# Splitting the expert weights once, and giving each weight slot its own run of tiles

## The chip, the cores and the metric

The kernel runs on one core of a Trainium2 chip. The core has a matrix engine (PE; its weight loads are listed as PEld), a vector engine (DVE), an activation engine (ACT), GpSimd (POOL) and a sync engine (SP) that mostly issues transfers. Each engine works through its own queue in order, and waits on semaphores where another engine or a transfer has to be done first. The metric is the device time of one execution in microseconds (us).

## The reference, cut to what matters

```python
# convolution along the sequence, by FFT of double length: x (8, 5696, 128), h (5696, 128)
y = irfft(rfft(x, 2*S, axis=1) * rfft(h, 2*S, axis=0)[None])[:, :S]
x = y.reshape(45568, 128)
# one expert of eight per token
logits = x @ w_gate + modality_bias[modality_id]
e_idx = argmax(logits, axis=1)
gate_w = softmax(logits)[range(N), e_idx]
for e in range(8):                      # w1[e]: 128 x 1024, w2[e]: 1024 x 128
    mask = e_idx == e
    out[mask] = gate_w[mask, None] * (maximum(x[mask] @ w1[e], 0) @ w2[e])
```

All arrays are float32. The kernel gets float32 accuracy from products in a shortened float32 format (float32r) by splitting an operand into a high part (a cast) and a low part (the rest), and adding three products: high by high, high by low, low by high. For the expert weights this split is what the change is about.

## The kernel before, in words

The convolution is a transform in four stages, over two groups of four batches. Stage 1 (`stage1`) transforms over 64 points and writes to a scratch in memory. Stages 2 and 3 (`stage23`, one step per k of 64) transform over the residues, multiply by the filter's transform and go back, into the scratches ua and ub. Stage 4 (`stage4`) goes back over k, three pairs of residues at a time; it makes the logits, picks the expert, ranks the tokens within their expert, and hands each of twelve columns of 128 tokens to `dispatch`, an indirect transfer from POOL (L297) that scatters the rows into `rows`, a scratch with a region for each expert.

The experts (`class Moe`) then work on tiles: 512 consecutive rows of one expert, or 256 in the last level. There are four levels, of 18, 18, 45 and 23 tiles: those that are full for sure after 27 pairs of residues of the first group, after the whole first group, after all, and then the short rest. For each level `table` works out on one partition, with small DVE operations, the first row and the expert of every tile and a flag that says whether the expert differs from that of the tile NSLOT places before. `load` brings a tile's rows (mrt, five buffers), and waits on SP for the scatters of the tile whose buffer it takes. `load_weights` reads the expert and the flag into registers of SP and loads 1 MiB of raw weights (w1 and w2 of the expert side by side) into one of two buffers raw, only if the flag is set. `split` makes the high part (ACT, L520) and the low part (DVE, L522; in the last level half of them on POOL) of a quarter of the weights, into one of three buffers slot; four such steps lie beside each tile's products, for the tile after it, whether raw was loaded anew or not. `prep` transposes the rows and splits them. `gemm1` makes the hidden rows (PE L546 to L548, ACT hh L551, DVE hl L552), `gemm2` the output (PE L568 to L570) two steps later, `finish` transposes back, multiplies by the gate (DVE L584) and scatters to out from POOL (L587).

A tile has eight steps (four if short), written out in `Moe.run`. `run_all` interleaves generators step by step: stages 2 and 3 of the first group with stage 1 of the second; stages 2 and 3 of the second group with stage 4 of the first 27 pairs; then the rest of stage 4 with the tiles. The framework's scheduler orders each engine's queue from this by priority and a simulated timeline, ahead of the run; only SP keeps the written order during the experts.

Of the kernel before, what the change touches and what calls it, by code (L numbers as in the profile page):

```python
# [10 lines left out]
F32 = mybir.dt.float32  # L11
F32R = mybir.dt.float32r
BF16 = mybir.dt.bfloat16
I32 = mybir.dt.int32
# [7 lines left out]
E, FF = 8, 1024  # L22
# [12 lines left out]
QA = 27     # pairs of residues of the first group that are dispatched before the experts start  # L35
HP = 1000   # how far the routing moves up in the scheduler's order
PACE = 2    # dispatches queued behind each product's last sum
S4R = 5     # steps of stage 4 per three of stages 2 and 3
RATE = 1.05  # steps of stage 4 per step of the experts
WH = 2      # every WH-th product goes back through whole float32 matmuls, the others through split ones  # L40
W0 = 52     # ... in the first group from this one on
LG = 3      # every LG-th set of logits goes through split operands
AHEAD = 6   # steps of stage 4 before the first fence


def full(q):
    """Tiles of TS rows that the tokens of the first q pairs of residues, over the groups' batches, fill for sure."""
    return (GB * (128 * q - 64) - E * (TS - 1)) // TS


# Tiles by level: full ones after a part of the first group, after the first group, after all, then short ones.
# [9 lines left out]
NSLOT = 2  # L61
# [3 lines left out]
def run_all(*gens):  # L65
    """Emit generators side by side; each is (generator, steps it takes per round)."""
    live = [[g, float(r), 0.0] for g, r in gens]
    while live:
        for it in list(live):
            it[2] += it[1]  # L70
            while it[2] >= 1.0:
                it[2] -= 1.0
                try:
                    next(it[0])
                except StopIteration:
                    live.remove(it)
                    break
# [3 lines left out]
def conv_moe(  # L81
# [3 lines left out]
    zd, hd, ua, ub, rows_d, out,  # L85
# [349 lines left out]
    def table(tp, lv, before):  # L435
# [17 lines left out]
        # Row of tile t of expert e: cur[e] + ts * (t - cum[e]), as a sum of steps at the experts' first tiles.  # L453
# [4 lines left out]
        it_i = t_(nt, "it_i", I32)  # L458
        nc.gpsimd.iota(it_i, pattern=[[1, nt]], base=0, channel_multiplier=0)
        it = t_(nt, "it")  # L460
        nc.vector.tensor_copy(it, it_i)
# [21 lines left out]
        if not last:  # L483
            # Rows of each expert in the first nt tiles.
            nc.vector.tensor_scalar(cum, cum, float(nt), None, op0=ALU.min)
            nc.vector.tensor_tensor(cnt, cum[:, 1:], cum[:, :E], op=ALU.subtract)
            nc.vector.scalar_tensor_tensor(cur, cnt, float(ts), cur, op0=ALU.mult, op1=ALU.add)
# [4 lines left out]
    class Moe:  # L492
        def __init__(self, wp, sp, pst, psh, pso):
            self.sp, self.pst, self.psh, self.pso = sp, pst, psh, pso
            self.raw = [wp.tile([128, 2, FF], F32, name=f"raw{i}") for i in range(NSLOT)]
            self.slots = [wp.tile([128, 2, 2, FF], F32R, name=f"slot{i}") for i in range(3)]
            self.st = {}
            self.tabs = {}
# [11 lines left out]
        def load_weights(self, t):  # L510
# [4 lines left out]
            nc.sync.dma_start(self.raw[t % NSLOT], w12_d[bass.ds(ex, 1)].rearrange("o p a f -> (o p) a f"), cond=ch > 0)  # L515

        def split(self, t, k):
            raw, w = self.raw[t % NSLOT], self.slots[t % 3]
            i, fs = k // 2, slice(k % 2 * (FF // 2), (k % 2 + 1) * (FF // 2))
            nc.scalar.copy(w[:, i, 0, fs], raw[:, i, fs])  # L520
            eng = nc.gpsimd if JOBS[t][0] == len(LEVELS) - 1 and k % 2 else nc.vector
            eng.tensor_tensor(w[:, i, 1, fs], raw[:, i, fs], w[:, i, 0, fs].bitcast(F32), op=ALU.subtract)  # L522
# [14 lines left out]
        def gemm1(self, t, f):  # L537
            w = self.slots[t % 3]
# [16 lines left out]
        def gemm2(self, t, f):  # L555
            w = self.slots[t % 3]
# [34 lines left out]
        def run(self):  # L591
# [11 lines left out]
            for k in range(4):  # L603
                self.split(0, k)
            self.prep(0)
            for g in range(len(steps) + LAG):
# [5 lines left out]
                if f == 0 and t + 2 < total:  # L612
                    self.load_weights(t + 2)
                if t < total:
                    self.gemm1(t, f)
                if g >= LAG:
                    self.gemm2(*steps[g - LAG][:2])
                if t + 1 < total:
                    if n == 4 or f % 2 == 1:
                        with tc.issue_after(self.st[t]["act"].ins):  # L620
                            self.split(t + 1, f * 4 // n)
# [12 lines left out]
    with tc.tile_pool(name="p4", bufs=2, space=PSUM) as ps4, \  # L634
            tc.tile_pool(name="p4l", bufs=1, space=PSUM) as ps4l:
        with tc.tile_pool(name="s2", bufs=2) as sp2, tc.tile_pool(name="p2x", bufs=3, space=PSUM) as psx, \
# [6 lines left out]
            run_all((stage23(1, sp2, psx, psu), 3), (stage4(0, sp4, ps4, ps4l, 0, QA, True), S4R))  # L643
            dispatch(len(queue))

        def fence():
            """Orders the loads of a level behind the dispatch before it."""
# [113 lines left out]
```

## Time and profile before

| | us |
|---|---|
| median of three timed runs | 2400.83 (2379.54 to 2401.71) |
| span of the profiled execution, first to last instruction | 2272.4 |
| own time of the profiled execution | the page gives only its span |
| mean granted clock of PE | 0.955 |
| busy: PE, DVE, ACT, POOL | 2068.7, 1751.5, 1394.7, 1242.3 |

On the trace's own clock stage 1 of the first group runs until about 236 us, stages 2 and 3 of the first group with stage 1 of the second until about 560, stages 2 and 3 of the second group with the first part of stage 4 until about 890, tiles beside the rest of stage 4 until about 1420, full tiles alone until about 2070 to 2095, and the 23 short tiles to the end.

How to read the lines that follow. The table of windows has a row for each stretch: its ends and length, then busy time and count of instructions for each engine, the granted clock (1.00 is full), the busy share of the transfer engines and their rate in GB/s. A group of instructions has the line, the engine, the operation, the tiles out<-in with their shapes and the count; then busy time, mean ns of one, idle time of the engine ahead of them and what ended it. A tile's row has the shortest, median and longest duration in ns, and the first and last start. A wait has who waited, for whom, the sum in us, how many times and the longest. A row of the timeline or of the chain has its start, its length in us and what ran; SPq is SP's queue.

### The profile page before, as it was taken

How to read it: one execution, taken by the hardware profiler on the slowest of the kernel's cores; microseconds unless marked ns; L12 is line 12 of the kernel's file. 1: busy time of each engine (PE TensorE's matmuls, PEld its weight loads, DVE VectorE, ACT ScalarE, POOL GpSimd, SP SyncE). 2: the span in 40 equal slices, each digit the busy share in tenths (PEclk: the TensorE clock that was granted, in tenths of full speed). 3: DMA queues.
4: the chain of work that ended last, by engine and by line, in shares of the span. 5: the costliest groups of instructions: out<-in, count | busy, mean ns of one | idle time of the engine just before them, and what ended most of it. 6: DMA issues, size and time to landing. Idle time of an engine off the chain costs nothing. (4 is left out here: it accounts for less than half of the span.)

```text
span 2272.4 us, 33999 instructions
## 1 busy us (share of the span) xinstructions
PE 2068.7 (91%) x9752; PEld 1537.7 (68%) x9752; DVE 1751.5 (77%) x2907; ACT 1394.7 (61%) x2496; POOL 1242.3 (55%) x1102
## 2 busy tenths in 40 slices
PE   6779899899888988989888998999999999999896
PEld 5655555445554545877766776888888888888886
DVE  6559999899889896778566777877777777777675
ACT  6547776546444545766666664666666666666674
POOL 2126665664787887754777777333333333334675
PEclk9999999899979996999999999999999999999998
DMA  9989989778767766443445423232112211112321
GB/s 325 332 294 314 325 287 297 209 243 273 219 190 212 219 196 205 142 135 100 139 123 160 147 83 103 81 100 64 47 60 63 65 62 44 46 43 90 127 81 46
DMA packets 195436, 357.48 MB, mean 157 GB/s; under 512 B 32438, under 2 KB 63514, under 8 KB 191409
## 3 DMA queue, kind: packets, MB, share of 16 engines
q1 hardware_dynamic: 150560, 270.52, 37.3%
q0 software_dynamic: 23520, 47.61, 6.3%
q10 hardware_dynamic: 21168, 37.17, 5.4%
q8 instruction: 78, 1.28, 0.2%
q14 instruction: 110, 0.89, 0.1%
HBM read 276.51 MB, written 157.43 MB: 191 GB/s over the span
## 5 line engine op out<-in xcount | busy, mean ns | idle before, releaser
L552 DVE SCALAR_TENSOR_TENSOR hl<-ph,hh 128x512 fp32r<-128x512 f32 x740 | 508.2, 689 | 257.6 <-ACT hh L551 248.9
L587 POOL DMA_INDIRECT out<-of,mrt x370 | 390.2, 1055 | 535.8 <-DVE of L584 427.2
L551 ACT ACTIVATE hh<-ph 128x512 fp32r<-128x512 f32 x740 | 443.1, 600 | 362.7 <-PE ph L548 354.8
L297 POOL DMA_INDIRECT rows<-rt,idx x360 | 401.7, 1116 | 121.6 <-issue 85.8
L270 POOL TENSOR_TENSOR t<-t,t 96x512 f32<-96x512 f32 x218 | 335.5, 1560 | 182.5 <-DVE t L263 163.4
L263 DVE TENSOR_TENSOR t<-px,hs 96x512 f32<-96x512 f32 x512 | 320.2, 675 | 26.0 <-ACT hs L223 10.5
L546 PE MATMUL ph<-mxh,slot 128*128 128x512 f32 (+1 forms) x832 | 322.1, 387 | 16.8 <-DVE hl L552 13.1
L568 PE MATMUL po<-hh,slot 128*128 128x512 f32 (+1 forms) x832 | 326.6, 393 | 9.5 <-ACT hh L551 9.3
L548 PE MATMUL ph<-mxh,slot 128*128 128x512 f32 (+1 forms) x832 | 312.4, 376 | 0.6 <-POOL slot L522 0.4
L569 PE MATMUL po<-hl,slot 128*128 128x512 f32 (+1 forms) x832 | 311.0, 374 | 0.0
L547 PE MATMUL ph<-mxl,slot 128*128 128x512 f32 (+1 forms) x832 | 310.8, 374 | 0.0
L570 PE MATMUL po<-hh,slot 128*128 128x512 f32 (+1 forms) x832 | 310.5, 373 | 0.0
L260 PE MATMUL px<-z,m 96*96 96x512 f32 x512 | 269.9, 625 | 21.6 <-issue 6.6
L522 DVE TENSOR_TENSOR slot<-raw,slot 128x512 fp32r<-128x512 f32 x370 | 265.3, 719 | 22.6 <-ACT slot L520 22.4
L520 ACT CAST slot<-raw 128x512 fp32r<-128x512 f32 x416 | 251.8, 614 | 23.8 <-DMA raw<-in_w 23.8
L546 PEld LDWEIGHTS ph<-mxh,slot 128*128 128x128 f32 x832 | 159.5, 192 | 43.3 <-DVE hl L552 18.3
L243 ACT COPY ut<-pu 90x512 f32<-90x512 f32 x256 | 144.5, 583 | 70.0 <-PE pu L238 25.8
L568 PEld LDWEIGHTS po<-hh,slot 128*128 128x128 f32 x832 | 159.1, 191 | 33.2 <-ACT hh L551 10.8
L548 PEld LDWEIGHTS ph<-mxh,slot 128*128 128x128 f32 x832 | 158.7, 191 | 31.6 <-POOL slot L522 0.8
L569 PEld LDWEIGHTS po<-hl,slot 128*128 128x128 f32 x832 | 158.7, 191 | 30.0 <-DVE hl L552 0.2
L570 PEld LDWEIGHTS po<-hh,slot 128*128 128x128 f32 x832 | 158.8, 191 | 29.6
L547 PEld LDWEIGHTS ph<-mxl,slot 128*128 128x128 f32 x832 | 159.1, 191 | 26.7
(153 smaller groups left out, 3477.8 us busy)
## 6 DMA issues: line engine op xcount, KB each, us to landing
raw<-in_w SPq DMA_DIRECT2D x104, 1024.0 KB
z<-z SPq DMA_DIRECT2D x256, 180.0 KB
z<-z SPq DMA_DIRECT2D x90, 320.0 KB
z<-z SPq DMA_DIRECT2D x90, 256.0 KB
ua<-ut SPq DMA_DIRECT2D x128, 180.0 KB
ub<-ut SPq DMA_DIRECT2D x128, 180.0 KB
mrt<-rows SPq DMA_DIRECT2D x81, 260.0 KB
u<-ua ACTq DMA_DIRECT2D x63, 256.0 KB
```

The source lines that it names most:

```text
L263: nc.vector.tensor_tensor(prod[i, j].rearrange("p (b d) -> p b d", d=D), px[:KP].rearrange("p (b d) -> p b d", d=D), hs[:, j, k % KH].unsq ...
L270: add = eng.tensor_tensor(y[:, i], y[:, i], prod[1, 1 - i], op=ALU.add if i else ALU.subtract)
L297: nc.gpsimd.indirect_dma_start(views[count[0] % NVIEW], bass.IndirectOffsetOnAxis(ap=idx[:, t:t + 1], axis=0), rt[:, t, :], None, bounds_c ...
L546: nc.tensor.matmul(po, w[:, 0, 0, fs], st["xh"], start=True, stop=False)
L547: nc.tensor.matmul(po, w[:, 0, 0, fs], st["xl"], start=False, stop=False)
L548: nc.tensor.matmul(po, w[:, 0, 1, fs], st["xh"], start=False, stop=True)
L551: st["act"] = nc.scalar.activation(hh, ph, AF.Relu)
L552: nc.vector.scalar_tensor_tensor(hl, ph, 0.0, hh.bitcast(F32), op0=ALU.max, op1=ALU.subtract)
L568: nc.tensor.matmul(po, w[:, 1, 0, fs], hh[:, cs], start=k == 0, stop=False)
L569: nc.tensor.matmul(po, w[:, 1, 0, fs], hl[:, cs], start=False, stop=False)
L570: nc.tensor.matmul(po, w[:, 1, 1, fs], hh[:, cs], start=False, stop=k == 7)
L587: nc.gpsimd.indirect_dma_start(oviews[(t * NSUB + c) % NVIEW], bass.IndirectOffsetOnAxis(ap=ri[:, c, D + 1:D + 2], axis=0), of[:, c, :], N ...
```

## The change

Between stages 2 and 3 of the second group and stage 4, a third generator, `presplit`, is interleaved, one step per round: in 16 steps (eight experts, w1 and w2) it loads 512 KiB of raw weights, casts the high part on ACT, subtracts on DVE and stores both parts, 1 MiB, to a new scratch w12s; its tile has one buffer, and ACT issues both transfers. `load_weights` now loads 2 MiB of ready parts from w12s straight into the slot, if the expert of the slot changes; raw and `split` are gone. NSLOT, the distance of the flag's comparison, goes from 2 to 3, so a slot keeps its weights from one of its tiles to the next. `table` numbers the tiles of a level in another order: tile j of the level is number (j % 3) * run + j // 3, with run the third part of the level's tiles rounded up, so each slot walks through a contiguous run of the experts. The call of `load_weights(t + 2)` moves from ahead of `gemm1` at step 0 of tile t to behind `gemm2` at step 1, where `gemm2` has just read the slot for the last time for tile t - 1.

```diff
-NSLOT = 2
+NSLOT = 3
...
-    zd, hd, ua, ub, rows_d, out,
+    zd, hd, ua, ub, rows_d, w12s, out,
...
+    def presplit(sp):
+        for e in range(E):
+            for a in range(2):
+                s = sp.tile([128, 2, FF], F32R, name="ws")
+                v = s.bitcast(F32)
+                nc.scalar.dma_start(v[:, 1], w12_d[e, :, a])
+                nc.scalar.copy(s[:, 0], v[:, 1])
+                nc.vector.tensor_tensor(s[:, 1], v[:, 1], v[:, 0], op=ALU.subtract)
+                nc.scalar.dma_start(w12s[e, :, a], v)
+                yield
...
-        it_i = t_(nt, "it_i", I32)
-        nc.gpsimd.iota(it_i, pattern=[[1, nt]], base=0, channel_multiplier=0)
+        it_i = t_(nt + NSLOT, "it_i", I32)[:, :-(-nt // NSLOT) * NSLOT]
+
+        run = -(-nt // NSLOT)
+        nc.gpsimd.iota(it_i, pattern=[[1, run], [run, NSLOT]], base=0, channel_multiplier=0)
         it = t_(nt, "it")
-        nc.vector.tensor_copy(it, it_i)
+        nc.vector.tensor_copy(it, it_i[:, :nt])
...
-            self.raw = [wp.tile([128, 2, FF], F32, name=f"raw{i}") for i in range(NSLOT)]
-            self.slots = [wp.tile([128, 2, 2, FF], F32R, name=f"slot{i}") for i in range(3)]
+            self.slots = [wp.tile([128, 2, 2, FF], F32R, name=f"slot{i}") for i in range(NSLOT)]
...
-            nc.sync.dma_start(self.raw[t % NSLOT], w12_d[bass.ds(ex, 1)].rearrange("o p a f -> (o p) a f"), cond=ch > 0)
-
-        def split(self, t, k):
-            raw, w = self.raw[t % NSLOT], self.slots[t % 3]
-            i, fs = k // 2, slice(k % 2 * (FF // 2), (k % 2 + 1) * (FF // 2))
-            nc.scalar.copy(w[:, i, 0, fs], raw[:, i, fs])
-            eng = nc.gpsimd if JOBS[t][0] == len(LEVELS) - 1 and k % 2 else nc.vector
-            eng.tensor_tensor(w[:, i, 1, fs], raw[:, i, fs], w[:, i, 0, fs].bitcast(F32), op=ALU.subtract)
+            nc.sync.dma_start(self.slots[t % NSLOT].bitcast(F32), w12s[bass.ds(ex, 1)].rearrange("o p a i f -> (o p) a i f"), cond=ch > 0)
...
             self.load(2)
-            for k in range(4):
-                self.split(0, k)
             self.prep(0)
...
-                if f == 0 and t + 2 < total:
-                    self.load_weights(t + 2)
                 if t < total:
                     self.gemm1(t, f)
                 if g >= LAG:
                     self.gemm2(*steps[g - LAG][:2])
+                if f == LAG - 1 and t + 2 < total:
+                    self.load_weights(t + 2)
                 if t + 1 < total:
-                    if n == 4 or f % 2 == 1:
-                        with tc.issue_after(self.st[t]["act"].ins):
-                            self.split(t + 1, f * 4 // n)
                     if f == (4 if n == 8 else 1):
                         self.prep(t + 1)
...
-            run_all((stage23(1, sp2, psx, psu), 3), (stage4(0, sp4, ps4, ps4l, 0, QA, True), S4R))
+            with tc.tile_pool(name="ws", bufs=1) as wsp:
+                run_all((stage23(1, sp2, psx, psu), 3), (stage4(0, sp4, ps4, ps4l, 0, QA, True), S4R), (presplit(wsp), 1))
```

More of the change, by code (lines that the diff above doesn't have):

```diff
@@ L537, in gemm1 @@
         def gemm1(self, t, f):
-            w = self.slots[t % 3]
+            w = self.slots[t % NSLOT]
             st = self.st[t]
@@ L555, in gemm2 @@
         def gemm2(self, t, f):
-            w = self.slots[t % 3]
+            w = self.slots[t % NSLOT]
             st = self.st[t]
@@ L755 @@
     args.append(scratch("rows", (NROWS, RW)))
+    args.append(scratch("w12s", (E, 128, 2, 2, FF)))
     args.append(nc.dram_tensor("out", (NTOK, D), F32, kind="ExternalOutput").ap())
```

## The prediction

> **What bounds the kernel now.** I read the page's first lines, then a table of windows cut where the instructions change character.
>
> ```profile
> span 2272.4 us, 33999 instructions
> PE 2068.7 (91%) x9752; PEld 1537.7 (68%) x9752; DVE 1751.5 (77%) x2907; ACT 1394.7 (61%) x2496; POOL 1242.3 (55%) x1102
> ```
> ```profile
> core 0: us, PE busy (x) PEld busy (x) DVE busy (x) ACT busy (x) POOL busy (x), PEclk, DMA share, GB/s
> 0.00:236.00 236.00, 177.42 (x802) 131.75 (x802) 161.90 (x195) 146.59 (x234) 73.39 (x89) 0.96 0.92 318
> 236.00:560.00 324.00, 296.35 (x980) 162.15 (x978) 301.62 (x380) 207.45 (x359) 192.80 (x134) 0.97 0.85 269
> 560.00:900.00 340.00, 297.45 (x1100) 171.25 (x1100) 291.63 (x504) 165.68 (x286) 270.96 (x216) 0.87 0.68 206
> ...
> 900.00:1420.00 520.00, 472.56 (x2568) 381.00 (x2569) 373.42 (x834) 335.06 (x617) 356.24 (x345) 0.95 0.41 129
> 1420.00:2070.00 650.00, 650.00 (x3004) 526.82 (x3004) 488.12 (x790) 412.09 (x751) 225.77 (x216) 1.00 0.20 60
> 2070.00:2272.40 202.40, 174.96 (x1303) 164.78 (x1301) 134.82 (x207) 127.81 (x253) 123.13 (x104) 0.95 0.28 92
> ```
>
> Four stages matter here. 560 to 900 (the second group's stages 2 and 3 beside the first part of stage 4; call it the front) has no full engine: DVE is busy 291.63 of 340 us, PE 297.45 at a granted clock of 0.87. 900 to 1420 mixes the rest of stage 4 with expert tiles; PE is idle for 520 - 472.56 = 47.4 us. 1420 to 2070 holds full tiles alone, and PE has no idle time at clock 1.00. From 2070 on come the 23 short tiles.
>
> The work that the change takes away shows in three groups:
>
> ```profile
> L522 DVE TENSOR_TENSOR slot<-raw,slot 128x512 fp32r<-128x512 f32 x370 | 265.3, 719 | 22.6 <-ACT slot L520 22.4
> L520 ACT CAST slot<-raw 128x512 fp32r<-128x512 f32 x416 | 251.8, 614 | 23.8 <-DMA raw<-in_w 23.8
> ```
> ```profile
> L522 POOL TENSOR_TENSOR slot<-raw,slot x46: 1272/1306/1704, 2085.8 to 2254.0; 128x512 fp32r<-128x512 f32 x46
> ```
>
> That is 265.3 us of DVE, 251.8 of ACT and 46 x 1.3 = 60 of POOL. It looks like a great deal, but an engine that isn't the last to be ready gives nothing back. So I ask of each stage what PE waited for, first in the mixed stage, then among the short tiles (2097 to 2255):
>
> ```profile
> PE py L349 <- ACT rt L345: 25.0, 8, 7.0
> PE pxt L581 <- ACT ot L573: 9.7, 2, 7.5
> PE po L568 <- ACT hh L551: 9.1, 3, 5.9
> PE ph L546 <- ACT slot L520: 1.8, 1, 1.8
> ```
> ```profile
> PE ph L546 <- DVE hl L552: 12.4, 13, 3.4
> PE ph L546 <- ACT slot L520: 1.7, 3, 1.1
> PE ph L548 <- POOL slot L522: 0.4, 1, 0.4
> ```
>
> These waits (45.6 and 14.5 us in the rows shown) are nearly the whole stock from which the change can earn while PE is loaded.
>
> **What goes.** In 1420:2070 the gain is zero: PE is busy 650.00 of 650 us. ACT and DVE merely become idler there.
>
> In the mixed stage I look for the cause of the ACT waits, since ACT takes its instructions in order:
>
> ```profile
> ACT rt L345 <- DMA rows<-rt,idx: 41.5, 10, 7.6
> ...
> ACT slot L520 <- DMA raw<-in_w: 15.6, 3, 9.0
> ```
> ```profile
> 1399.29 0.62 ACT L520 CAST slot<-raw 128x512 fp32r<-128x512 f32 x1 [9.02 <-DMA raw<-in_w]
> 1399.81 0.58 ACT L573 COPY ot<-po 128x512 f32<-128x512 f32 x1
> ```
> ```profile
> 1391.32 0.34 SPq L507 DMA_DIRECT2D mrt<-rows  x1
> 1393.24 0.33 SPq L515 DMA_DIRECT2D raw<-in_w  x1
> ```
>
> A weight load was issued only at 1393.24, behind a row load on SP. The cast that needs it held ACT for 9.02 us, and the copy of ot queued behind it held PE's transpose. So pxt's 9.7 us and the 1.8 us of slot belong to the splits: 11.5 us go. The 41.5 us for scattered rows (the rt buffer comes free when its scatters have landed) have nothing to do with weights; py's 25.0 and most of hh's 9.1 stay. What is late next is the load itself, now 2 MiB. The old need came at step 1 of the tile before, where its split starts; the new one at step 0 of the tile itself, 7 of 8 steps later. A full tile in the PE-bound stage takes 650.00 / (3004 / 56) = 12.1 us (48 products and 8 transposes a tile, 3004 of them in the stage), so that is 10.6 us more room. A 1 MiB load took 5.15 us in the quiet part:
>
> ```profile
> 2116.53 5.15 DMA raw<-in_w
> ```
>
> Bounds for 2 MiB are 5.15 (all latency) and 10.3 (all bytes); I take 8, so about 3 us of the 10.6 are spent. The added wait (SP holds the load of tile t+2 until PE has read slot (t+2)%3 for tile t-1) has only row loads behind it on SP, which are already three tiles ahead. Sum here: -11.5 us; from -5, if one load still comes late, to -29, if half of the 34 us behind rt and hh goes too because ACT catches up faster.
>
> Among the short tiles the same argument holds with smaller numbers. hl waits on DVE behind a subtract, that behind a cast on ACT, that behind the load. Of the 14.5 us in the three rows I count 12 as gone: a short tile has four steps and one split per step, so the need moves by about one step less than a tile (some 5 us of a tile of (2255 - 2097) / 23 = 6.9 us), more than the 3 us that the bytes add. At the very end POOL no longer has a 1.3 us subtract between its last scatters: 1 us more. Sum: -13, from 0 (every load late) to -18. By the routing computed from the reference (experts 1, 3 and 5 take nearly all tokens) the table asks for about 30 loads of 1 MiB before and 16 of 2 MiB after, so the traffic stays the same and the count of possible late loads halves.
>
> The split of the very first tile goes too, but the load ahead of it grows by about as much as the split took; PE has stage 4 to do meanwhile: 0.
>
> **What comes.** The new generator runs in the front: 16 steps, each with a 512 KiB load, an ACT copy and a DVE subtract of 128x1024, and a 1 MiB store, both transfers issued by ACT. The nearest rows are this stage's own:
>
> ```profile
> L336 DVE TENSOR_TENSOR ul<-u,uh 128x1024 fp32r<-128x1024 f32 x32 | 41.8, 1305 | 11.5 <-ACT uh L335 10.2 <-PE pl L396 1.3
> L230 DVE TENSOR_TENSOR yl<-t,yh 96x1024 fp32r<-96x1024 f32 x25 | 40.4, 1615 | 20.1 <-ACT yh L276 20.1
> ```
> ```profile
> L335 ACT CAST uh<-u 128x1024 fp32r<-128x1024 f32 x31 | 32.5, 1048 | 1.8 <-DMA hs<-hd 1.6
> ```
>
> DVE gets 16 x 1.305 = 20.9 us (25.8 at yl's 1.615), ACT 16.8 and 32 issues. Lower end: DVE ran at 301.62/324 = 93% in the stage before, and (291.6 + 20.9) / 0.93 = 336 us fits into the 340, so the cost can be 0. Upper end: DVE's share stays what it is, and the stage grows by 340 x 20.9/291.6 = 24 us, or 30 at 1.615. I take +18, nearer the upper end, because DVE was already full for 60 us of this stretch:
>
> ```profile
> 800.00:840.00 40.00, 35.45 (x124) 19.21 (x122) 40.00 (x68) 18.60 (x33) 30.78 (x23) 0.91 0.70 214
> 840.00:860.00 20.00, 15.93 (x49) 7.95 (x48) 20.00 (x36) 9.61 (x16) 18.52 (x12) 0.78 0.49 157
> ```
>
> and because POOL, the other adder of this stage, is busy 270.96 of 340 and its adds are stretched when DVE is busy (mean 1493 ns here, 1257 at the least):
>
> ```profile
> L270 POOL TENSOR_TENSOR t<-t,t 96x512 f32<-96x512 f32 x75 | 110.5, 1493 | 30.5 <-DVE t L263 19.9 <-DVE rb L470 5.3 <-DVE idx L416 4.0
> ```
> ```profile
> L270 POOL TENSOR_TENSOR t<-t,t x218: 1257/1286/4417, 165.0 to 866.0; 96x512 f32<-96x512 f32 x109
> ```
>
> The Trainium skill's "VectorE: DVE Perf Modes", section Two Vector instructions with no wait between them, speaks against the change here: a vector instruction with two SBUF inputs reads one of them through an interface that it shares with GpSimd, and the new subtract is such an instruction. The stretched rows agree with it; if each of the 16 subtracts cost POOL the 0.24 us between 1493 and 1257 on top of its own time, the sum by the page would be 4 us worse, 2398.
>
> The transfers add 16 x 1.57 = 25 MB. At the 269 GB/s that 0.85 of the engines moved in the stage before, 206 GB/s x 340 us + 25 MB = 95 MB need 353 us at that rate, 299 us at the 318 GB/s of the first window. So transfers come near their limit without passing it. I cost them at nothing, covered by z loads that are issued two steps ahead; uncovered, the stage grows to 353, +13, which is inside DVE's bounds and not on top of them.
>
> **Sum.** +18 - 11.5 - 0 - 13 = -6.5 us. The page gives this execution only its span of 2272.4; the median of the three timed runs, 2400.83, is 128.4 above that. I leave that difference untouched and forecast 2394. One per cent is 24 us, about what a measurement of this kernel can tell from no change; the timed runs themselves lie 22 us apart.
>
> **Rivals.**
>
> *Faster: the front hides the split.* DVE has 340 - 291.63 = 48 us of holes, ACT half the stage. Then +18 becomes 0, and the lighter ACT and DVE let the mixed stage recover some of the 34 us behind rt and hh, say 15: 2401 - 11.5 - 13 - 15 = 2361. For it: ACT's share. Against it: the two full DVE windows, and POOL's scatters, which set rt free and don't change. Chance 0.28.
>
> *Slower: ACT stalls on the new transfers.* ACT takes its queue in order, and each step puts two waits for a DMA into it: the copy waits for the load, and the next load waits until the store has left the single buffer. The order is fixed ahead; wherever the transfer is slower than that order assumed, everything behind it on ACT (uh, yh, ut, rt) stands. The trace has such a wait in this stage, and its size:
>
> ```profile
> ACT rt L345 <- DMA rows<-rt,idx: 16.0, 5, 6.0
> ```
>
> that is 3.2 us each; in the mixed stage 41.5 us of them became 25.0 us of PE waits in py, 0.6. One per step costs 16 x 3.2 x 0.6 = 31 us, both 61. I take 36: 2394 + 36 = 2430. It decides from 31 us of passed-on stall upward, one stall per step: 2394 + 31 is where 1% ends. For it: transfers go from 206 towards 290 GB/s just there. Against: ACT is idle half of the stage. Chance 0.22.
>
> *The change doesn't do what it says in the short tiles.* Their loads stay late, since SP still issues them behind row loads that wait for scatters:
>
> ```profile
> SPq L507 <- DMA out<-of,mrt: 101.9, 22, 9.2
> ```
>
> Then seven loads of 2 MiB each cost 3 us more instead of nothing: +13 + 21 on my sum, 2428. Chance 0.04. The forecast (2377 to 2425) keeps 0.46.
>
> **Numbers.** Faster 0.28, same 0.46, slower 0.26. The range takes in the faster rival's centre and the slower rival's, with a few us for its spread: 2356 to 2440.
>
> **What the new profile would show.** Right: no raw; the front some 18 us longer, with DVE above 90%; the full-tile stage at PE 100% and 12.1 us a tile; PE's waits in the mixed stage short of pxt's 9.7 but with py behind rt unchanged; few us of waits of ph in the short tiles; POOL without subtracts. Wrong: ACT's waits for the split's load or its buffer above 30 us in the front (slower), a front no longer than 345 us (faster), a ph that waits for the weight load itself (last rival), or a front whose engines are re-ordered so much that its length has another cause.

## The result and the profile after

The kernel after takes 2418.2 us (median of 8 runs, 2413.21 to 2437.16), the kernel before 2396.57 beside it (8 runs, 2379.54 to 2406.26): a ratio of 1.0106, 95% interval 1.0073 to 1.0138, so 22 us slower by the medians and 25 by the ratio. The forecast was 2394, a little faster.

The kernel was timed on six occasions; on five the kernel before took 2397 to 2405 us (medians), and on the last, on another chip, 2271.16 (19 runs). The profile that the prediction was read from, with a span of 2272.4, is of the second kind; the change was timed on the first. Ratios below always compare runs of one chip. Own time is the span and some 2 us (2421.28 us for the profiled execution after, span 2419.0).

The page after opens so:

```profile
span 2419.0 us, 33191 instructions
PE 2124.4 (88%) x9752; PEld 1554.2 (64%) x9752; DVE 1549.9 (64%) x2553; ACT 1214.5 (50%) x2096; POOL 1145.5 (47%) x1056
```

DVE has 201.6 us less to do than in the first profile of before, ACT 180.2, POOL 96.8, and the counts fit the change: 354 instructions fewer on DVE (370 out, 16 in), 400 on ACT (416 out, 16 in), 46 on POOL. Still the span is longer. So that like is compared with like, before was profiled again on a chip of the slower kind (own time 2401.37 us, span 2399.6). The table of windows, now cut at the first expert product, at the first product of tile 36, at that of tile 81 (the first short tile) and at the end; before again, then after:

```profile
core 0: us, PE busy (x) PEld busy (x) DVE busy (x) ACT busy (x) POOL busy (x), PEclk, DMA share, GB/s
560.00:916.50 356.50, 298.52 (x1100) 170.95 (x1100) 288.19 (x503) 165.67 (x287) 269.88 (x218) 0.85 0.65 199
916.50:1676.70 760.20, 635.80 (x3151) 499.26 (x3152) 473.42 (x1018) 415.22 (x761) 396.06 (x386) 0.90 0.32 103
1676.70:2221.60 544.90, 544.90 (x2522) 441.75 (x2520) 405.53 (x630) 346.08 (x632) 189.20 (x182) 1.00 0.18 55
2221.60:2399.60 178.00, 151.14 (x1203) 144.92 (x1201) 119.60 (x183) 113.79 (x227) 114.60 (x96) 0.96 0.27 89
```
```profile
560.00:912.30 352.30, 306.54 (x1106) 172.28 (x1104) 298.05 (x519) 175.98 (x297) 261.08 (x204) 0.87 0.77 243
912.30:1697.90 785.60, 646.66 (x3190) 503.33 (x3191) 402.28 (x889) 352.43 (x626) 399.80 (x403) 0.89 0.33 107
1697.90:2242.70 544.80, 544.80 (x2521) 441.65 (x2521) 306.73 (x450) 262.85 (x451) 174.89 (x180) 1.00 0.18 55
2242.70:2419.00 176.30, 154.12 (x1202) 144.28 (x1200) 80.00 (x139) 70.36 (x139) 48.55 (x50) 0.97 0.30 101
```

The front is 4.2 us shorter, the mixed stage 25.4 longer, the 45 full tiles 0.1 shorter, the short level 1.7 shorter: together the 19.4 us between the spans. The loss stands in the mixed stage, in which PE's idle time grows from 760.20 - 635.80 = 124.4 us to 138.9 and its busy time from 635.8 to 646.7, although DVE and ACT each have over 60 us less to do there. One execution of each is a thin base, so I take in the profiles whose PE works through this stage in exactly the same order. For the order of before they are before again, jitter1 and order2 (the last two are told below): 760.2, 758.2 and 762.1 us. For that of after they are after, after again and after_noload3: 785.6, 802.6 and 799.4. The loss of 25.4 is the smallest of these differences; the largest is 44.

The same rows of the profile that the prediction used:

```profile
901.40:1546.60 645.20, 599.16 (x3151) 483.44 (x3152) 471.43 (x1018) 414.17 (x761) 400.66 (x387) 0.96 0.39 122
1546.60:2091.50 544.90, 544.90 (x2522) 441.74 (x2520) 405.42 (x630) 346.09 (x632) 189.22 (x182) 1.00 0.18 55
2091.50:2272.40 180.90, 153.46 (x1204) 147.41 (x1201) 119.50 (x183) 114.03 (x227) 114.27 (x96) 0.95 0.27 87
```

It is one kernel with one order of instructions, and the mixed stage takes 645.2 us in one profile and 760.2 in the other: 78.4 us more idle time of PE and 36.6 more busy time at a clock of 0.90 instead of 0.96. That is 115.0 of the 127.2 us between the two spans.

What this idle time looks like, in the timeline of after (weight loads of PE and SP's queue left out; ... stands for rows left out):

```profile
1146.38 0.39 PE L554 MATMUL ph<-mxh,slot 128*128 128x512 f32 x1
1146.61 0.39 PE L575 MATMUL po<-hl,slot 128*128 128x512 f32 x1
1146.79 0.97 POOL L297 DMA_INDIRECT rows<-rt,idx  x1 [0.30 <-issue]
1146.84 0.40 PE L576 MATMUL po<-hh,slot 128*128 128x512 f32 x1
...
1154.45 0.97 POOL L297 DMA_INDIRECT rows<-rt,idx  x1 [0.30 <-issue]
1157.06 0.69 DVE L590 TENSOR_TENSOR of<-pxt,mrt 128x512 f32<-128x512 f32 x1 [11.30 <-remote]
1157.81 1.12 PE L535 MATMUL pxt<-ident,mrt 128*128 128x128 f32 x4 [10.57 <-DVE of L590]
...
1159.87 0.60 ACT L557 ACTIVATE hh<-ph 128x512 fp32r<-128x512 f32 x1 [14.83 <-PE pxt L535]
...
1162.27 0.63 PE L554 MATMUL ph<-mxh,slot 128*128 128x512 f32 x1
1162.69 0.63 PE L575 MATMUL po<-hl,slot 128*128 128x512 f32 x1
```

POOL is at the end of an unbroken run of 20 scatters, from 1130.2 to 1155.4 us. DVE, ACT and PE all stand for 10 to 15 us. ACT's hh has had its product since about 1147, and starts at 1159.87; DVE's of goes on 1.6 us after the last scatter of the run. I call this a pause. After it PE's products start 0.42 us apart (1162.27, 1162.69) instead of 0.23 (1146.61, 1146.84), because its clock has dropped:

```profile
1130.00:1145.50 15.50, 13.13 (x59) 9.73 (x58) 6.67 (x13) 5.55 (x10) 11.67 (x12) 1.00 0.12 39
1145.50:1157.00 11.50, 1.51 (x6) 0.86 (x5) 0.26 (x1) 0.00 (x0) 7.78 (x8) 0.68 0.25 76
1157.00:1170.00 13.00, 7.24 (x16) 4.29 (x16) 2.77 (x4) 1.78 (x3) 9.38 (x11) 0.63 0.21 66
```

The clock is 0.63 in the window after the pause. The Trainium skill, "TensorE: Matmul & The Clock Gate", Part 1, has the rule for it: an idle window of about 3.4 us halves the clock, and a busy one of that length gives it back. The trace agrees (10.57 us idle, then products 0.42 us apart): a pause costs its own length and then products at about half speed for some us.

To see how regular this is, I took from each trace the unbroken runs of scatters, to rows and to out, between 900 and 1560 us (the next one starts within 0.5 us of the end of the last, with no other work of POOL between), and for each position in such a run the share of time in which PE was idle, from the start of a scatter to that of the next:

| position in the run | before, first profile | before again | after | ratio 0.9 | ratio 1.2 |
|---|---|---|---|---|---|
| 1 to 4 | 0.01 | 0.03 | 0.12 | 0.07 | 0.04 |
| 5 to 8 | 0.06 | 0.10 | 0.16 | 0.13 | 0.04 |
| 9 to 12 | 0.06 | 0.45 | 0.45 | 0.05 | 0.09 |
| 13 to 16 | 0.21 | 0.49 | 0.85 | 0.07 | 0.15 |

The first and the last two columns are of the faster kind of chip. On the slower kind PE stands about half of the time or more from the ninth scatter of a run on; on the faster it does not, in runs of up to 52 scatters.

The semaphore records of the traces show what the engines stand for. In the pause above, DVE's of starts 0.02 us after a signal of PE (an update of its semaphore) that is recorded at 1157.04, and PE had ended its last instruction before that at 1147.24: the signal came some 10 us late. I took all signals by which PE, ACT and DVE tell of a finished instruction in the mixed stage, and counted one as late when no record follows within 0.5 us of the instruction's end. On the slower kind 541 of 2354 are late in before again and 488 of 2095 in after; on the faster kind 2 of 2354 in the first profile, 3 of 2094 at ratio 0.9 and none of 2085 at ratio 1.2. In after 3% are late outside the runs of scatters, 31% during a run's first four scatters and over half from the fifth on; ahead of the first scatter of all no signal is late in any of these traces. So on the slower kind the signals between the engines come late, or are recorded late, while POOL scatters, and a long run makes all engines stand. Why only there is open.

### The profile page after: what moved, and what is told of

Same layout as the page of the kernel before. It is cut to its first block, busy times and chain, and to the rows that moved or that the text cites. A ratio compares the mean times of both kernels' runs of the same rounds, so it can differ in the third digit from the quotient of the medians.

```text
span 2419.0 us, 33191 instructions
## 1 busy us (share of the span) xinstructions
PE 2124.4 (88%) x9752; PEld 1554.2 (64%) x9752; DVE 1549.9 (64%) x2553; ACT 1214.5 (50%) x2096; POOL 1145.5 (47%) x1056
## 4 chain that ended last, share of the span: by engine, by line
issue 31%; PE 16%; POOL 8%; another core or an unknown queue 4%; DVE 2%; ACT 1%; DMA 1%; POOLq 0%; ACTq 0%; DVEq 0%; SPq 0%
POOL out L593 7%; PE py L342 2%; PE ph L552 2%; PE ph L554 2%; PE po L574 2%; PE ph L553 2%; PE po L575 2%; PE po L576 2%; PE pl L356 1%; PE py L349 1%; POOL rows L297 1%; DVE hl L558 0%; DVE ul L336 0%; ACT hh L557 0%
## 5 line engine op out<-in xcount | busy, mean ns | idle before, releaser
L593 POOL DMA_INDIRECT out<-of,mrt x370 | 371.7, 1004 | 773.2 <-DVE of L590 591.8
L297 POOL DMA_INDIRECT rows<-rt,idx x360 | 394.3, 1095 | 145.3 <-issue 94.2
L270 POOL TENSOR_TENSOR t<-t,t 96x512 f32<-96x512 f32 x218 | 328.4, 1528 | 193.4 <-DVE t L263 167.0
L552 PE MATMUL ph<-mxh,slot 128*128 128x512 f32 (+1 forms) x832 | 334.3, 402 | 12.2 <-DVE hl L558 10.6
L554 PE MATMUL ph<-mxh,slot 128*128 128x512 f32 (+1 forms) x832 | 314.2, 378 | 0.0
L260 PE MATMUL px<-z,m 96*96 96x512 f32 x512 | 277.5, 639 | 12.1 <-DVE t L263 7.8
L243 ACT COPY ut<-pu 90x512 f32<-90x512 f32 x256 | 144.2, 582 | 96.8 <-PE pu L238 34.3
L230 DVE TENSOR_TENSOR yl<-t,yh 96x1024 fp32r<-96x1024 f32 x90 | 163.3, 1817 | 34.2 <-ACT yh L276 29.5
L553 PEld LDWEIGHTS ph<-mxl,slot 128*128 128x128 f32 x832 | 161.4, 194 | 23.6 <-issue 0.4
L336 DVE TENSOR_TENSOR ul<-u,uh 128x1024 fp32r<-128x1024 f32 x90 | 110.2, 1225 | 87.5 <-ACT uh L335 41.6
```

The source lines that it names most:

```text
L270: add = eng.tensor_tensor(y[:, i], y[:, i], prod[1, 1 - i], op=ALU.add if i else ALU.subtract)
L297: nc.gpsimd.indirect_dma_start(views[count[0] % NVIEW], bass.IndirectOffsetOnAxis(ap=idx[:, t:t + 1], axis=0), rt[:, t, :], None, bounds_c ...
L552: nc.tensor.matmul(po, w[:, 0, 0, fs], st["xh"], start=True, stop=False)
L553: nc.tensor.matmul(po, w[:, 0, 0, fs], st["xl"], start=False, stop=False)
L554: nc.tensor.matmul(po, w[:, 0, 1, fs], st["xh"], start=False, stop=True)
L593: nc.gpsimd.indirect_dma_start(oviews[(t * NSUB + c) % NVIEW], bass.IndirectOffsetOnAxis(ap=ri[:, c, D + 1:D + 2], axis=0), of[:, c, :], N ...
```

## The experiments

Each is told with its edit, its expectation as it was put on record, and what came out. "Mixed" is the time from the first expert product to that of tile 36 in the profiled execution: 760.2 us before (before again), 785.6 after. All but the last two ran on the slower kind of chip, so their ratios are against a before of about 2400 us.

**Both kernels profiled once more.** No edit.

> The kernel before, unchanged, once more with a profile, because the profile that the prediction was read from has a span of 2272.4 us and its timed runs lie at 2380 to 2406. If that profile was of an ordinary execution, this one shows a span near 2272 again and 47 us of idle PE between 900 and 1420. If it was an unusually short one, this one shows about 2390, and the extra 120 us stand as PE idle time in the mixed stage (tiles beside stage 4), since the full-tile stage cannot be slower without PE showing idle time.

> The changed kernel, unchanged, once more with a profile. Theory A (the long PE pauses of its mixed stage, ten of over 7 us, belong to the order of the queues): the same pauses at the same instructions, span 2410 to 2440. Theory B (they are accidents of one execution): pauses elsewhere, in other sizes.

Before 2401.37 us, after 2444.47, with mixed stages of 760.2 and 802.6. Of the nine pauses of PE over 4.5 us in the mixed stage of after, six come ahead of the same product in after again (two of them at about 1005 to 1015 and 1147 to 1158 us), the others do not. So the order of the instructions decides for the most part where the pauses fall, but not alone: one order gave 785.6 and 802.6 us.

**The split alone, added to before and never read** (pre_only), **and the change with the split cut to one expert** (no_pre).

```diff
 pre_only, on before:
+            run_all((stage23(1, ...), 3), (stage4(0, ...), S4R), (presplit(wsp), 1))
 no_pre, on after:
-        for e in range(E):
+        for e in range(1):
-            nc.sync.dma_start(... w12s[bass.ds(ex, 1)] ..., cond=ch > 0)
+            nc.sync.dma_start(... w12s[0:1] ..., cond=ch > 0)
```

> The kernel before with the new split into the scratch added and nothing else changed: the tiles still load raw weights and split them each time, and nobody reads the scratch. Theory A (the front pays for the split): 2397 plus 18 to 36, so 2415 to 2433, and the expert tiles start that much later. Theory B (the front hides it and the loss lies in the mixed stage): 2397 plus 0 to 10, the first expert product at most 10 us later.

> The changed kernel with the split into the scratch cut to one expert of eight (2 of the 16 steps), and every tile loads that expert's weights: the loads keep their sizes, conditions and places, the output is not the reference's. Theory A (the front pays for the split): 14 of 16 steps go, so 2418 minus 16 to 32, 2386 to 2402. Theory B (the loss lies in the mixed stage): 2418 minus 0 to 9.

pre_only: 2433.17 us, 1.0105 [1.0049, 1.016]. no_pre: 2421.19, 1.0072 [1.0041, 1.0103]. So adding the split costs 12 to 38 us, about what the whole change costs, but taking 14 of its 16 steps out of the change gives back only some 8 us (1.0106 against 1.0072), which the intervals don't tell from nothing; its mixed stage takes 779.8 us, with 40 pairs of residues done ahead of the first tile. pre_only pays in the same place as after:

```profile
560.00:920.70 360.70, 310.89 (x1069) 175.28 (x1068) 303.77 (x507) 174.28 (x293) 262.52 (x207) 0.83 0.74 235
920.70:1704.50 783.80, 644.15 (x3210) 504.50 (x3208) 480.43 (x1038) 421.15 (x773) 409.21 (x399) 0.90 0.32 101
```

The front grew by 4.2 us against before again, the mixed stage by 23.6. Counting the products of L342, stage 4 has done 34 pairs of residues in before when stages 2 and 3 read their last z (the last product of L260), and 28.8 in pre_only and after. By the first expert product it is 39 pairs against 37. The split hardly lengthens the front, it displaces stage 4, which has to be made up for beside the tiles.

**Halves of the split, on before:** its transfers alone (pre_dma: two loads of 512 KiB and the store of 1 MiB per step) and its arithmetic alone (pre_calc, on one loaded tile). The edit is shown against pre_only.

```diff
 pre_dma:
-                nc.scalar.copy(s[:, 0], v[:, 1])
-                nc.vector.tensor_tensor(s[:, 1], v[:, 1], v[:, 0], op=ALU.subtract)
+                nc.scalar.dma_start(v[:, 0], w12_d[e, :, a])
 pre_calc:
-                nc.scalar.dma_start(v[:, 1], w12_d[e, :, a])
...
+                if e == 0 and a == 0:
+                    nc.scalar.dma_start(raw, w12_d[e, :, a])
-                nc.scalar.dma_start(w12s[e, :, a], v)
```

> The kernel before with the new generator's transfers alone: 16 times two loads of 512 KiB and a store of 1 MiB to a scratch that nobody reads, no cast and no subtract. The split alone cost 1.05%. If the transfers and ACT's waits for them displace the stage 4 work: slower by 0.7 to 1.2%, with 28 to 30 pairs of residues through stage 4's first product when stages 2 and 3 end, in place of 34. If the arithmetic does: within 0.3%.

> The kernel before with the new generator's arithmetic alone: one load of raw weights, then 16 casts and 16 subtracts of 128x1024, no stores. If the arithmetic displaces the stage 4 work: slower by 0.5 to 1.1%. If the transfers do: within 0.3%.

pre_dma: 2424.74 us, 1.0086 [1.0051, 1.0121]. pre_calc: 2440.72, 1.0142 [1.0097, 1.0186]. In both, stage 4 keeps its 34 pairs and the front is what grows (first tile at 935.5 and 945.6 us, 916.5 before). Each half alone costs about as much as the whole: the parts do not add up. The queues are ordered anew for each of them, and that is my reading of it, not shown.

**Any small edit at the same place:** sixteen tiny clears, or one, as a third generator; **and the new numbering of the tiles alone**, on before.

```diff
 jitter16 and jitter1 (n = 16, 1):
+        for _ in range(n):
+            nc.vector.memset(sp.tile([128, 8], F32, name="tiny"), 0.0)
+            yield
 order2:
-        nc.gpsimd.iota(it_i, pattern=[[1, nt]], base=0, channel_multiplier=0)
+        nc.gpsimd.iota(it_i, pattern=[[1, run], [run, NSLOT]], base=0, channel_multiplier=0)
```

> The kernel before with a third generator in the front that does nothing of use: 16 steps, each one DVE memset of 128x8 (about 0.06 us each, 1 us in all). Theory C (the order that the scheduler happened to find for the kernel before is a lucky one, and any edit loses it): slower by 0.5 to 1.5%, with the loss between the first tile and tile 36, as for the split alone. Theory A (the split's own work costs the time): within 0.4% of before.

> The same with a single such memset. Theory C: slower by 0.5 to 1.5% again, by another amount. Theory A: within 0.4% of before.

> The kernel before with the new numbering of tiles alone, two runs side by side, one for each raw buffer; splits and loads of raw weights stay. Theory F: nothing changes, 2390 to 2410. Theory G (the order costs: two or three experts at a time make loads fall where the tiles are short): slower by 0.3 to 0.8%.

jitter16: 2392.39 us, 0.9973 [0.9934, 1.0012]. jitter1: 2400.04, 1.0029 [0.9993, 1.0066]. order2: 2395.96, 0.9994 [0.9966, 1.0023]. Of these only jitter16 changes the order in which PE works: its queue differs from before's, and its mixed stage takes 766.6 us. In jitter1 and order2 PE's queue is that of before, product for product, so they say nothing on another order. Before does not owe its time to an order that every edit destroys, by that one case, and numbering the tiles in two runs costs nothing.

**Scatters.** Two columns at a time instead of four (before_d2, after_d2); a fourth buffer rt (after_rt4); no scatters to out for the first 24 tiles (after_noout, which leaves those rows of the output unwritten).

```diff
 before_d2, after_d2:
-                dispatch(4)
+                dispatch(2)
 after_rt4:
-            rt = sp.tile([128, T, RW], F32, name="rt", bufs=3)
+            rt = sp.tile([128, T, RW], F32, name="rt", bufs=4)
 after_noout:
-            for c in range(ns):
+            for c in range(ns if t >= 24 else 0):
```

> The kernel before with two row scatters per step of the unpaced stage 4 in place of four, so that POOL's runs of scatters become shorter. In the runs so far PE stood 44 to 90% of the time from the ninth scatter of an unbroken run on, and 3 to 18% during the first four. Theory D (long runs of scatters on POOL hold the other engines): PE's idle time beside stage 4 falls by 30 us or more, 2405 becomes 2375 or less. Theory E (POOL is merely late as a whole, and the runs only mark where): idle time unchanged, 2395 to 2415.

> The changed kernel with the same edit. Theory D: 2425 becomes 2390 or less. Theory E: 2410 to 2440.

> The changed kernel with four buffers rt of scattered rows in place of three. Theory H (PE stands late in POOL's runs of scatters because ACT waits for an rt whose twelve scatters are not out yet): one group more of room, PE's idle time beside stage 4 falls by 30 us or more, 2420 becomes 2390 or less. Theory I (it stands because POOL itself, or the semaphores, are held up while it issues): no change, 2410 to 2435.

> The changed kernel without the scatters to out of its first 24 tiles (96 of POOL's scatters beside stage 4; those rows of the output stay unwritten). Theory I: the runs of scatters become shorter and POOL idler by 120 us, PE's idle time falls by 30 us or more, 2420 becomes 2385 or less. Theory J (PE and the interleaving of steps set the pace, POOL only marks it): 2405 to 2430.

before_d2: 2390.06 us, 0.9993 [0.9957, 1.0028]; after_d2: 2419.09, 1.0118 [1.0048, 1.0188]. Smaller portions change nothing. after_rt4: 2469.42, 1.0302 [1.0249, 1.0354]: with a buffer more, stage 4's scatters may follow one another more closely. Its first tile comes at 935.0 us, 22.7 later than in after, and its mixed stage takes 805.3. after_noout: 2364.6, 0.9876 [0.9833, 0.992].

```profile
916.30:1637.10 720.80, 628.43 (x3190) 493.57 (x3191) 401.55 (x889) 352.85 (x626) 293.00 (x303) 0.93 0.32 104
```

96 scatters fewer shorten the mixed stage by 64.8 us against after, 0.67 us each, although POOL was busy only half of the stage (399.80 of 785.60). That fits the late signals, but it is no clean test: with these scatters the waits of of and of the row loads for them go as well.

**The splits out of the tiles of before** (nosplit: three slots are split once at the start from one expert, and the tiles use those; the raw loads stay). **Useless work in their place in after** (after_dummy: a cast and a subtract of the same shapes, into a buffer nobody reads, in the full tiles).

```diff
 nosplit, on before:
-                    if n == 4 or f % 2 == 1:
-                        with tc.issue_after(self.st[t]["act"].ins):
-                            self.split(t + 1, f * 4 // n)
 ...
 after_dummy, on after:
+                    if n == 8 and f % 2 == 1:
+                        with tc.issue_after(self.st[t]["act"].ins):
+                            self.dummy(t, f // 2)
```

> The kernel before without its splits inside the tiles: the three slots are split once, all from the first raw buffer, ahead of the first tile (8 casts and subtracts more there), the raw loads go on as they were, and every tile uses those weights; the output is not the reference's. Theory A of the prediction (the splits cost 11 us beside stage 4 and 13 among the short tiles): 2399 becomes 2370 to 2385. Theory F (ACT and DVE have room for the splits everywhere, so taking them away changes nothing): 2390 to 2405.

> The changed kernel with useless casts and subtracts put where the splits of the full tiles stood (four of each per full tile, the same sizes, written to a spare buffer; none in the short tiles). Theory K (the scheduler's order of the mixed stage, made with or without the splits' durations in its plan, sets that stage's length): the stretch from the first tile to tile 36 shrinks from 781 to 803 us towards 760 to 775, though more work is done, and 2419 becomes 2395 to 2410. Theory L (more work can't help): 2415 to 2435.

nosplit: 2387.69 us, 0.9945 [0.9912, 0.9977]. after_dummy: 2411.53, 1.0041 [1.0004, 1.0079]. First nosplit, then after_dummy:

```profile
905.60:1691.20 785.60, 643.55 (x3151) 506.67 (x3152) 403.66 (x883) 352.37 (x626) 384.01 (x386) 0.88 0.31 100
2236.00:2391.40 155.40, 142.80 (x1202) 141.53 (x1200) 80.21 (x139) 70.82 (x139) 48.57 (x50) 0.97 0.31 101
```
```profile
911.80:1672.80 761.00, 640.65 (x3191) 501.30 (x3192) 476.94 (x1032) 419.80 (x770) 412.03 (x399) 0.91 0.34 108
```

These two runs say most. Taking the splits out of before makes its mixed stage 25.4 us longer (it begins 10.9 us earlier and ends 14.5 later), although the front's new work and the new loads are not in it. Putting as much useless work back into after makes the stage 24.6 us shorter, 761.0, as before, though it makes up for as much of stage 4 as after does. DVE and ACT do 75 and 67 us more there, and PE gets through earlier. The timed runs give less: from 1.0106 to 1.0041, some 16 us, with intervals that just touch; the profiled execution of after_dummy, 2396.59 us, is among the fastest of its twelve (2396.07 to 2430.61). So the presence of the work, and not the time that it takes, is worth some 16 to 25 us in this stage. Both runs change the order of the queues along with the work: PE's differs between before and nosplit, and between after and after_dummy. That the order does it is my reading; that the work slows ACT and DVE and so spreads the scatters during the run is a rival that these runs don't exclude. nosplit is faster than before nevertheless, because its short level takes 155.4 us instead of 178.0.

**No weight loads in the last level of after** (after_noload3: the short tiles compute with weights left in the slots).

```diff
-                if f == LAG - 1 and t + 2 < total:
+                if f == LAG - 1 and t + 2 < total and JOBS[t + 2][0] < len(LEVELS) - 1:
```

> The changed kernel without the weight loads of the last level; its tiles use whatever weights lie in the slots, so the output is not the reference's. The queue of PE then alternates six products up, six down; with the loads it has blocks of twelve and seventeen. Theory M (the plan reckons a 2 MiB load for each short tile, taken or not, and the blocks cost time in every tile): a short tile takes 6.1 us in place of 7.1, the last level 16 to 20 us less, 2419 becomes 2398 to 2405. Theory N (only the few loads really taken cost time, where they are late): 5 us less at most.

2419.47 us, 1.006 [1.0028, 1.0092].

```profile
2263.50:2417.80 154.30, 142.08 (x1202) 141.22 (x1200) 80.04 (x139) 71.85 (x139) 48.68 (x50) 0.97 0.12 34
```

The short level drops from 176.3 to 154.3 us. Of these 22 us the timed runs show about 11 (1.0106 to 1.006, not clear of the intervals), and the profiled execution loses them ahead of it: its first tile comes 6.9 us later than in after, and its mixed stage, with the same order of PE, takes 13.8 more (799.4). In after, short tiles alternate between 6.9 and 7.8 us from the eighth on, whether a load is taken there or not, and PE's queue has blocks of 12 products up (ph) and 17 down (po). In nosplit and here the tiles take 6.1 us each and the blocks alternate 6 and 6. The order looks as if every short tile waited for a load of 2 MiB, the conditional ones included, and so the 22 us that the splits' removal is worth here go back into it. That the order and not the few loads really taken is the cost rests on the regular alternation; the loads and the order went together in this run.

**The ratio at which stage 4 and the tiles are interleaved,** in after.

```diff
-RATE = 1.05
+RATE = 0.9      (after_rate0.9; 1.2 in after_rate1.2)
```

> The kernel after, with the ratio of the interleave of the rest of stage 4 with the tiles at 0.9 instead of 1.05: fewer steps of stage 4 for each step of the tiles. Theory of the fixed queue order: the 25 us that the mixed stage lost come from how the two kinds of work are put into the queues, so the ratio moves the mixed stage by some 20 us, and one of the two ratios tried may bring it back towards 760 us and the time towards 2395. Rival, the loss is in the work itself (fewer pairs of stage 4 done ahead, the scatters' pauses): the mixed stage stays between 780 and 800 us and the time between 2410 and 2430 at either ratio.

> The kernel after, with the ratio of the interleave at 1.2 instead of 1.05: more steps of stage 4 for each step of the tiles, so that stage 4 ends earlier and its scatters stand closer together. Theory of the fixed queue order: the mixed stage moves by some 20 us against the kernel after, in the other direction than at 0.9 or in the same. Rival, the loss is in the work itself: 780 to 800 us in the mixed stage and 2410 to 2430 in all.

This was the chip of the faster kind. after_rate0.9: 2264.67 us, 0.9967 [0.9947, 0.9987]. after_rate1.2: 2274.66, 1.0022 [1.0003, 1.004]. For the question whether the ratio brings the lost 25 us back on the slower kind, both are inconclusive. But they show what the change does where there are no pauses; ratio 0.9, then 1.2:

```profile
560.00:915.50 355.50, 307.02 (x1117) 173.59 (x1115) 306.94 (x522) 178.66 (x300) 262.39 (x205) 0.86 0.76 242
915.50:1546.60 631.10, 598.37 (x3190) 484.73 (x3191) 399.77 (x889) 350.81 (x626) 408.13 (x404) 0.96 0.41 134
2091.40:2267.60 176.20, 154.17 (x1202) 144.53 (x1200) 79.88 (x139) 70.39 (x139) 48.66 (x50) 0.98 0.30 101
```
```profile
560.00:910.00 350.00, 309.43 (x1099) 173.51 (x1098) 308.41 (x519) 175.75 (x295) 256.09 (x205) 0.86 0.77 243
910.00:1552.40 642.40, 599.82 (x3197) 485.72 (x3194) 401.75 (x889) 351.79 (x626) 402.55 (x403) 0.96 0.42 132
2097.10:2273.50 176.40, 154.23 (x1202) 144.59 (x1201) 79.90 (x139) 70.46 (x139) 48.67 (x50) 0.97 0.30 101
1208.00:1227.00 19.00, 17.84 (x86) 13.56 (x86) 14.04 (x28) 13.71 (x25) 15.31 (x13) 0.82 0.44 135
1227.00:1246.70 19.70, 17.15 (x89) 14.09 (x88) 9.53 (x23) 8.29 (x16) 15.13 (x16) 0.91 0.67 212
```

The last two rows are one run of 28 scatters: PE is busy for 35.0 of its 38.7 us. Against the first profile of before, ratio 0.9 gives +14.1 in the front, -14.1 in the mixed stage, -0.1 and -4.7 in the short level, -4.8 us in all; ratio 1.2 gives +8.6, -2.8, -0.2 and -4.5, +1.1 in all. The kernel after with its own ratio of 1.05 was not run on this chip.

## Why the prediction was wrong

**The difference left untouched.** This step failed: "the median of the three timed runs, 2400.83, is 128.4 above that. I leave that difference untouched". A span and the own time of its execution differ by some 2 us, so some 126 of the 128.4 us were time that this profile did not show. In before again 115.0 of the 127.2 us lie in the mixed stage, in its pauses. The change acts just there. The table of waits of before shows it. The prediction rested on 45.6 us of waits for four named causes; before again, PE's longest sums between 900 and 1500 us (where the first profile has the same four rows as the prediction) are

```profile
PE po L568 <- ACT hh L551: 21.0, 9, 7.0
PE py L349 <- ACT rt L345: 20.5, 6, 4.9
PE po L568 <- issue: 19.4, 7, 8.4
PE pl L402 <- ACT tot L398: 15.8, 4, 8.2
```

and neither pxt behind ot nor a wait of over 1.6 us for slot is in the rows.

**Mixed stage, -11.5.** Wrong in sign for what was timed: +25.4, or up to 44 by the other profiles. The waits that I priced were a true row of an execution without pauses, and there the step held: with ratio 1.2 the waits behind ot and slot are gone and py behind rt stays, as the prediction said.

```profile
PE py L349 <- ACT rt L345: 30.8, 9, 10.0
PE pl L368 <- ACT ys L362: 7.2, 1, 7.2
PE po L574 <- ACT hh L557: 3.6, 4, 2.7
```

The stage's own differences, -14.1 and -2.8, stand around the -11.5, at other ratios than the change's own. On the slower kind the saving is lost in the pauses: in after pxt even waits 7.4 us behind ot, which before again does not have. nosplit and after_dummy show that the missing splits bring a loss of this size; whether by the new order of the queues or by the missing brake is open. pre_only loses as much in this stage with all splits in place, and in after the two do not add up. Why after meets more of a pause is open too. Its share of 0.85 at positions 13 to 16, against 0.49, rests on 24 scatters.

**Front, +18.** Within its bounds in price, wrong in place. pre_only measured +12 to +38 us; the front itself became 4.2 us shorter in after, on the faster kind 8.6 and 14.1 longer, and DVE is busy 85% of it, not over 90. I had put all sixteen steps behind 560 us; the scheduler put them earlier:

```profile
L437 ACT CAST ws<-ws x16: 1031/1045/1058, 402.1 to 726.4; 128x1024 fp32r<-128x1024 f32 x16
L438 DVE TENSOR_TENSOR ws<-ws x16: 1203/1212/3354, 403.4 to 729.4; 128x1024 fp32r<-128x1024 f32 x16
```

16 x 1.212 us is 19.4 of DVE, as priced. Stage 4 gave way, and its debt fell due in the mixed stage: 39 more instructions and 10.9 us more of PE's busy time (after against before again). The prediction read the Trainium skill's "VectorE: DVE Perf Modes", section Two Vector instructions with no wait between them, as speaking for 4 us on POOL's adds; before again, and after:

```profile
L270 POOL TENSOR_TENSOR t<-t,t 96x512 f32<-96x512 f32 x218 | 335.5, 1559 | 177.2 <-DVE t L263 160.1
```
```profile
L270 POOL TENSOR_TENSOR t<-t,t 96x512 f32<-96x512 f32 x218 | 328.4, 1528 | 193.4 <-DVE t L263 167.0
```

Over the run they became no longer, so nothing of these 4 us appears here. With the split's arithmetic alone (pre_calc) their mean is 1600 ns, so the point is not settled either way.

**Full tiles, 0.** Right: 544.9 and 544.8 us, PE without idle time.

**Short tiles, -13.** Right that the splits cost time there, and even too little: nosplit gains 22.6 us. But after gains 1.7, on the faster kind 4.5 and 4.7. I counted the 2 MiB loads only when taken, 16 of them; by after_noload3 the order seems made for all that might be. The mis-sized term is what the change adds here, some 20 us and not the 3 us per load that I hid.

**Rivals.** "ACT stalls on the new transfers" had the right sign and nearly the right size (2430), but by luck, for its mechanism is not there. By its own numbers its 290 GB/s should be 280; 243 were measured. ACT's waits for the split's load, and the one behind its store, are

```profile
ACT ws L437 <- DMA ws<-in_w: 8.1, 5, 2.4
ACT hs L223 <- DMA w12s<-ws: 3.4, 1, 3.4
```

that is 11.5 us in six waits, far below the 31 us from which it decides. "Loads stay late" was near the truth for the short tiles, but, as far as after_noload3 goes, in the order and not in the transfers. That 2418.2 lies between 2356 and 2440 is luck too: the ends came from these rivals, and the loss has another place.

## What to carry to other kernels

Compare the profiled span with the timed runs before anything else: here they differed by 128 us, the profile showed another kind of execution than the one that was timed, and the missing time had a place. Where a scheduler orders the queues ahead of the run, work that is taken away is also a new order, so try the removal alone and the same removal with useless work in its place before pricing it. Look whether an edit changes the order at all: one that doesn't can't test it. A conditional load that is seldom taken may still be paid for at every place by the order made around it.

## What the runs showed of the hardware

The same kernel takes 2271 or about 2400 us, by the chip or the occasion (which of the two was not separated); 115 of 127 us of the difference lie in one stage, where on the slower kind PE stands idle 45 to 85% of the time from the ninth scatter of an unbroken run on. A scatter occupies POOL for 0.97 us on both kinds (median of L297), so its own duration does not tell them apart, and neither do its transfers: the time of their packets is 6.3% of the first profile's span and 6.0% of the longer one of before again, 143 and 144 us of 16 transfer engines. What differs is the signals: on the slower kind about half of those from PE, ACT and DVE are recorded over 0.5 us late from the fifth scatter of a run on, on the faster kind almost none. Why is open. A pause of about 10 us also halves PE's clock for some us after it, with products 0.42 instead of 0.23 us apart.
